# A kernel whose instruction order comes from an emission clock: SyncE's queue and each landing are put into the clock, the weight sums' rows are laid out anew and stored in two parts, and the first loads change places

## The chip, the cores and the metric

One core of one Trainium2 chip. The metric is the device time of one execution in microseconds (us), lower is better. A ratio is the mean time of one kernel's fast runs over the mean of the other's fast runs of the same rounds, so it is not quite the ratio of the medians that stand beside it. Engines in the profile: PE is TensorE's products, PEld its weight loads, DVE is VectorE, ACT is ScalarE, SP is SyncE, which issues the DMAs.

## The reference

Two layers of local attention and gated MLP over 2048 tokens, with shared weights:

```python
def reference(A_x, A_wqkv, A_wo, B_x, B_w1, B_w3, B_w2):
    # _A_ref: qkv = x @ wqkv, 32 heads of 32; each token attends to 8 tokens,
    #         2 apart, backwards; softmax; @ wo
    # _B_ref: h = silu(x @ w1) * (x @ w3); h @ w2      (1024 -> 3584 -> 1024)
    x = A_x
    x = x + _A_ref(_layernorm(x, axis=-1), A_wqkv, A_wo)
    x = x + _B_ref(_layernorm(x, axis=-1), B_w1, B_w3, B_w2)
    x = x + _A_ref(_layernorm(x, axis=-1), A_wqkv, A_wo)
    x = x + _B_ref(_layernorm(x, axis=-1), B_w1, B_w3, B_w2)
    return x
```

## The kernel before

Tokens go in four chunks of 512. Each engine executes its stream strictly in the order in which the program emits it, and that order is decided while the program is built, by a **clock of guesses**: `now` holds where TensorE, VectorE and ScalarE would stand, and VectorE's background work (norms, sums, values, scores) is emitted in front of an urgent operation only if the guess says it ends by then.

```python
    MM, TABLE, DMA = 0.216, 1.3, 2.5
    now = dict(pe=23.6, dve=15.0, act=24.5, table=None)
    x_at = [12.5, 21.5, 38.0, 44.0]          # when each chunk of x is believed there
    ...
    def background(until):
        while True:
            for queue in (norms, adds, values, scores):
                s = head(queue)
                if s is not None and max(now["dve"], s[1]) + s[0] <= until:
                    take(queue)
                    break
            else:
                return
```

A transfer is guessed by a constant: q, k and v are there 2.5 us after the later of the request and the store; a transposed tile 3.0 us after VectorE.

```python
            turned.append(max(now["dve"] + 3.0, turned[-1] + 1.5))
    ...
        qks[l, h] = qT, kT, max(now["dve"], qkv_at[l, h // R, 1]) + DMA
```

From the third unit on (a unit is one chunk of one layer), gate and up products use seven sums of weight blocks instead of eight blocks. ScalarE and VectorE make them during the first two units: a pass over the tile measures its size, a tiny product spreads the size, ScalarE writes scaled copies into a block, VectorE subtracts, and the block is stored to DRAM.

```python
        elif slot == 2:
            measure(u, g, w, junk)        # ScalarE, 3.6 us
        elif slot == 5:
            scales(u, g)                  # the "size" product on TensorE
            copies(u, g, w, 0)            # ScalarE writes block 0
    ...
    t_d = [[dram.tile([P, 2, 7 * KT // 2 * P], FP16, ...) ...]]
        nc.sync.dma_start(t_d[m][g][:, a, :], b.rearrange("p b k c -> p (b k c)"))
```

Three names recur. A *gather* is the small product with which TensorE collects the sums of scores that VectorE has made (`L` from `psm`). An *addition* is a sum of two results on VectorE for which the next `st` product, one of the gate and up products, waits (`st` from `st` and `big`). A *size product* spreads the measured size of a weight tile (`size`).

## Time and profile before

| | |
|---|---|
| median | 1632.05 us (1631.71 to 1632.39) |
| span of the profiled run | 1633.2 us |
| TensorE busy | 1586.3 us |
| VectorE busy | 1220.5 us |
| DMA share | 72% |

Three lines that the prediction does not show. The first is the page's share of the chain that ended last, by engine; the second is of ScalarE's waits (who, for what: us, times, longest); the third of the page's DMA issues (count, size of each, median us to landing).

```profile
PE 69%; DVE 18%; DMA 8%; ACT 2%; issue 1%; SPq 1%; DVEq 0%; ACTq 0%
```

```profile
ACT big L747 <- DMA t_d<-big: 21.5, 8, 7.2
```

### The profile page before, as it was taken

What the parts mean: (1) busy time and instruction counts of PE and PEld (TensorE: products, weight loads), DVE (VectorE), ACT (ScalarE), POOL (GpSimd) and SP (SyncE); (2) the same over time, 40 slices, a digit from 0 to 9 for tenths busy, and PEclk for the clock granted to TensorE, in tenths of its full rate; (3) what the DMA queues carried; (4) which work ended last, traced back from release to release, by engine and by line L of the source; (5) the groups of instructions that cost most, each with busy time, mean ns of one, the idle gap of its engine ahead of it and who ended that gap; (6) DMA issues with size and microseconds to landing.
All of it is one profiled execution on the core that took longest, in us unless ns stands there. A gap on an engine that the chain in (4) does not pass through costs nothing.

```text
span 1633.2 us, 24503 instructions
## 1 busy us (share of the span) xinstructions
PE 1586.3 (97%) x9844; PEld 1015.4 (62%) x9844; DVE 1220.5 (75%) x2180; ACT 647.9 (40%) x1002; POOL 3.4 (0%) x16
## 2 busy tenths in 40 slices
PE   9799999999899899999999999999999999999999
PEld 7566644444344477575675756757667667676866
DVE  4788887988889699898688977898389885434423
ACT  4243374546635236142452333514235223332421
POOL 0000000000000000000000000000000000000000
PEclk9999999999999999999999999999999999999999
DMA  8555758686948879577687867767878576867954
GB/s 260 158 174 133 202 179 286 187 268 192 305 136 277 268 251 286 195 260 233 217 259 238 266 222 234 241 236 250 269 216 299 193 257 219 266 232 254 318 181 143
DMA packets 298786, 377.91 MB, mean 231 GB/s; under 512 B 71472, under 2 KB 234672, under 8 KB 298544
## 3 DMA queue, kind: packets, MB, share of 16 engines
q1 hardware_dynamic: 298528, 376.22, 72.2%
q8 instruction: 77, 1.26, 0.3%
q14 instruction: 37, 0.30, 0.1%
q10 hardware_dynamic: 144, 0.13, 0.0%
HBM read 305.53 MB, written 55.05 MB: 221 GB/s over the span
## 4 chain that ended last, share of the span: by engine, by line
PE 69%; DVE 18%; DMA 8%; ACT 2%; issue 1%; SPq 1%; DVEq 0%; ACTq 0%
PE st L796 24%; PE acc L927 21%; PE ps L703 12%; PE po L651 6%; DVE tm L562 3%; DVE pr L478 3%; DMA xnT<-xn 2%; PE pg L901 2%; DVE tm L402 2%; PE pu L910 2%; DVE pr L402 2%; DMA t_d<-big 2%; DVE st L209 2%; DMA w3t<-in_B_w_dram 1%; DMA kT<-qkv_d 1%
## 5 line engine op out<-in xcount | busy, mean ns | idle before, releaser
L927 PE MATMUL acc<-w2t,hT 128*128 128x512 bf16 (+1 forms) x1804 | 391.1, 378 | 0.9 <-DMA w2t<-in_B_w_dram 0.9
L703 PE MATMUL ps<-xnT,wqkv 128*128 128x512 f16 (+1 forms) x1472 | 326.5, 383 | 0.0
L927 PEld LDWEIGHTS <-hT 128*128 128x128 bf16 x1804 | 176.2, 98 | 209.0 <-issue 1.9
L796 PEld LDWEIGHTS <-early 128*128 128x128 f16 x2688 | 263.9, 98 | 41.7 <-issue 2.0
L703 PEld LDWEIGHTS <-wqkv 128*128 128x128 bf16 x1472 | 211.1, 144 | 112.3 <-issue 7.6
L796 PEld LDWEIGHTS <-late 128*128 128x128 f16 x2016 | 197.5, 98 | 43.4 <-issue 18.9
L478 DVE TENSOR_TENSOR pr<-qT,kT 128x2048 bf16<-128x2048 bf16 x128 | 155.7, 1216 | 55.2 <-DMA kT<-qkv_d 55.2
L707 ACT CAST big<-ps 128x512 bf16<-128x512 f32 x184 | 106.2, 586 | 228.1 <-PE ps L703 222.7
L796 PE MATMUL st<-xnT,late 128*128 128x256 f16 x1344 | 175.8, 274 | 4.9 <-DVE big L844 4.6
L796 PE MATMUL st<-big,early 128*128 128x256 f16 x1344 | 173.4, 274 | 1.2 <-ACT st L822 1.2
L562 DVE TENSOR_TENSOR tm<-At,vT 128x2048 bf16<-128x2048 bf16 x128 | 155.7, 1216 | 17.2 <-ACT At L535 17.2
L796 PE MATMUL st<-xnT,early 128*128 128x256 f16 x1344 | 167.8, 274 | 0.0
L822 ACT COPY st<-st 128x512 f32<-128x512 f32 x84 | 48.2, 574 | 300.9 <-PE st L796 297.8
L937 DVE TENSOR_TENSOR x_sb<-x_sb,acc 128x512 bf16<-128x512 bf16 x129 | 87.2, 677 | 91.3 <-PE acc L927 90.6
L402 DVE TENSOR_TENSOR pr<-pr 128x1024 bf16<-128x1024 bf16 (+1 forms) x256 | 136.9, 550 | 0.4
L402 DVE TENSOR_TENSOR tm<-tm 128x1024 bf16<-128x1024 bf16 (+1 forms) x256 | 136.7, 549 | 0.3
L651 PE MATMUL po<-wo,oT 128*128 128x512 bf16 x512 | 116.9, 382 | 0.0
L910 PE MATMUL pu<-xnT,w3t 128*128 128x512 f16 x448 | 105.9, 379 | 2.5 <-DMA w3t<-in_B_w_dram 2.4
L901 PE MATMUL pg<-xnT,w1t 128*128 128x512 f16 x448 | 107.2, 382 | 0.3 <-DMA w1t<-in_B_w_dram 0.3
L834 DVE TENSOR_TENSOR st<-st,big 128x512 f32<-128x512 f32 x84 | 58.2, 693 | 63.9 <-ACT big L831 63.7
L810 DVE SCALAR_TENSOR_TENSOR hT<-st,down_scale,sg 128x512 bf16<-128x512 f32 x126 | 92.8, 744 | 12.1 <-PE st L796 12.1
L805 ACT ACTIVATE sg<-st,down_scale 128x512 bf16<-128x512 f32 x126 | 86.9, 690 | 32.5 <-PE st L796 31.8
(120 smaller groups left out, 1256.6 us busy)
## 6 DMA issues: line engine op xcount, KB each, us to landing
early<-t_d SPq DMA_DIRECT2D x84, 1024.0 KB, 7.0
late<-t_d SPq DMA_DIRECT2D x84, 768.0 KB, 6.4
w2t<-in_B_w_dram SPq DMA_DIRECT2D x48, 1024.0 KB, 7.7
wqkv<-in_A_wqkv_dram SPq DMA_DIRECT2D x28, 1024.0 KB, 7.8
t_d<-big SPq DMA_DIRECT2D x28, 896.0 KB, 5.0
qkv_d<-big SPq DMA_DIRECT2D x92, 256.0 KB, 2.5
w1t<-in_B_w_dram SPq DMA_DIRECT2D x14, 1024.0 KB, 7.6
w3t<-in_B_w_dram SPq DMA_DIRECT2D x14, 1024.0 KB, 10.1
```

What stands on the lines that cost most here:

```text
L402: nc.vector.tensor_tensor(b[:, 0:m, :], b[:, 0:m, :], b[:, m:2 * m, :], op=ALU.add)
L478: V.tensor_tensor(pr[:], qT[:], kT[:, :, k0:k0 + TCH], op=ALU.mult)
L562: V.tensor_tensor(tm[:], At[:], win, op=ALU.mult)
L651: nc.tensor.matmul(ps[:], lhsT=oT[:, t, j * P:(j + 1) * P], rhs=wo[:, t, hh * 512:(hh + 1) * 512], start=(t == 0), stop=(t == KT - 1))
L703: nc.tensor.matmul(ps[:], lhsT=ws[kk // KH][:, kk % KH, t::KT], rhs=xnT[:, kk, :], start=(kk == 0), stop=(kk == KT - 1))
L707: nc.scalar.copy(sgt[:, t - t0, :], ps[:])
L796: nc.tensor.matmul(out[:, a, :], lhsT=w[:, a, blk, k, :], rhs=rhs[:, k, :], start=start and a == 0 and k == 0, stop=k == KQ - 1, skip_grou ...
L810: nc.vector.scalar_tensor_tensor(hT[:, f:f + 2, t0:t0 + HT], src, inv, gates[g, q][:], op0=ALU.mult, op1=ALU.mult)
L901: nc.tensor.matmul(pg[:], lhsT=w1t[:, kk, fi * P:(fi + 1) * P], rhs=xnT[:, kk, :], start=(kk == 0), stop=(kk == KT - 1))
L910: nc.tensor.matmul(pu[:], lhsT=w3t[:, kk, fi * P:(fi + 1) * P], rhs=xnT[:, kk, :], start=(kk == 0), stop=(kk == KT - 1))
L927: nc.tensor.matmul(acc[:], lhsT=hT[:, f - f0, j * P:(j + 1) * P], rhs=w2ts[(f - f0) // 8][:, (f - f0) % 8, q0:q0 + step], start=(f == f0), ...
L937: nc.vector.tensor_tensor(xs, xs, acc[:], op=ALU.add)
```

## The change

The intent is that the clock know SyncE's queue and each DMA's landing, that weights, transposes, q, k and v be believed there when the queue would deliver them, that x be there early, and that the sums lie in DRAM as rows of 8 KB (early) and 6 KB (late) per partition.

```diff
-    MM, TABLE, DMA = 0.216, 1.3, 2.5
-    now = dict(pe=23.6, dve=15.0, act=24.5, table=None)
+    MM, TABLE = 0.216, 1.3
+    now = dict(pe=23.6, dve=15.0, act=24.5, table=None, sp=11.0, dma=26.0)
-    x_at = [12.5, 21.5, 38.0, 44.0]
+    x_at = [12.5, 21.5, 24.5, 27.5]
+    def dma(kb, ready=0.0, issue=0.45):
+        now["sp"] = max(now["sp"], ready, now["dma"] - 9.0) + issue
+        now["dma"] = max(now["dma"], now["sp"] + 0.2) + kb / 380
+        return now["dma"] + 1.3
 ...
-            turned.append(max(now["dve"] + 3.0, turned[-1] + 1.5))
+            turned.append(dma(420, max(now["dve"], free), 1.3))
 ...
-        load_x(1)
+        for c in range(1, NCH):
+            load_x(c)
 ...
-        qks[l, h] = qT, kT, max(now["dve"], qkv_at[l, h // R, 1]) + DMA
+        qks[l, h] = qT, kT, load_part(kT, l, 1, h * TCH, True)     # load_part returns dma(540, ...)
 ...
     def weight(kind):
+        now["pe"] = max(now["pe"], w_at[used[0]])
 ...
-        nc.sync.dma_start(t_d[m][g][:, a, :], b.rearrange("p b k c -> p (b k c)"))
+        nc.sync.dma_start(t_d[m][g][:, 4 * a:4 * (a + 1)], b[:, 0:4])
+        nc.sync.dma_start(t_d[m][g][:, 8 + 3 * a:8 + 3 * (a + 1)], b[:, 4:7])
 ...
-                then = (lambda: (load_weight(), load_weight()), lambda: load_x(2), lambda: load_x(3))
+                then = (None, lambda: (load_weight(), load_weight()))
```

Cut: `dma()` calls beside the other loads and stores, the believed time of the first q store, the loads' new views of the sums, and the bookkeeping of free transposed tiles.

More of the change, by code (lines that the diff above doesn't have):

```diff
@@ L192 @@
     down_scale = const.tile([P, 2, NG], FP32, name="down_scale")
-    t_d = [[dram.tile([P, 2, 7 * KT // 2 * P], FP16, name=f"t_d{m}_{g}") for g in range(NG)] for m in range(2)]
+    t_d = [[dram.tile([P, 14, KT // 2, P], FP16, name=f"t_d{m}_{g}") for g in range(NG)] for m in range(2)]
     qkv_d = [[dram.tile([P, KT, S], BF16, name=f"qkv_d{l}_{i}") for i in range(3)] for l in range(2)]
@@ L226, in norm_apply @@
         xnT = xnTs[key]
+        free = xnT_free.get(list(xnTs)[list(xnTs).index(key) - 2], 0.0)
         mv, sd, ready = moments[key, r]
@@ L248 @@
     turned = [0.0] * 3
+    xnT_free = {}
     moments = {}
@@ L389, in first_q @@
                     nc.sync.dma_start(q_rows[:, 4 * i:4 * i + 4, 0:CH], hT[:, 4 * i:4 * i + 4, :])
-        qkv_at[0, 0, 0] = now["act"] + DMA / 2
+        qkv_at[0, 0, 0] = 28.0
     def tree(n, mul, dst):
@@ L434, in load_part @@
             nc.sync.dma_start(tl[:], qkv_d[l][which][:, :, tok0 - (HALO if halo else 0):tok0 + TCH])
+        return dma(540, max(now["dve"] if which < 2 else 0.0, qkv_at[l, tok0 // CH, which]))
     def load_qk(l, h):
@@ L441, in load_qk @@
         load_part(qT, l, 0, h * TCH, False)
-        load_part(kT, l, 1, h * TCH, True)
-        qks[l, h] = qT, kT, max(now["dve"], qkv_at[l, h // R, 1]) + DMA
+        qks[l, h] = qT, kT, load_part(kT, l, 1, h * TCH, True)
     def load_v(l, h):
@@ L448, in load_v @@
         vT = qkvp.tile([P, KT, HALO + TCH], BF16, name="vT")
-        load_part(vT, l, 2, h * TCH, True)
-        vs[l, h] = vT, max(now["dve"], qkv_at[l, h // R, 2]) + DMA
+        vs[l, h] = vT, load_part(vT, l, 2, h * TCH, True)
     pe_queue = []
@@ L588 @@
             seq += [("qkv", which, h) for which in range(3) for h in range(2)]
-    w_tiles, due, used = [], [], [0]
+    w_tiles, w_at, due, used = [], {}, [], [0]
     def load_weight(pieces=1):
@@ L601, in load_weight @@
                                   wqkv_v[:, n * KH + k0:n * KH + k0 + step, i * D:(i + 1) * D])
+            at = dma(1024, now["pe"] if len(w_tiles) > 5 else 0.0)
         elif kind == "junk":
             w = wp.tile([P, KT, FG * P], BF16, name="junk", tag="w")
+            at = 0.0
         elif kind in ("early", "late"):
@@ L606, in load_weight @@
             w = wp.tile([P, 2, 4 if early else 3, KT // 2, P], FP16, name=kind, tag="w")
-            v = t_d[i][n][:].rearrange("p a (b k c) -> p a b k c", b=7, k=KT // 2)
-            nc.sync.dma_start(w[:], v[:, :, 0:4] if early else v[:, :, 4:7])
+            v = t_d[i][n][:, 0:8] if early else t_d[i][n][:, 8:14]
+            nc.sync.dma_start(w[:], v.rearrange("p (a b) k c -> p a b k c", a=2))
+            at = dma(1024 if early else 768, now["pe"])
         elif kind == "w2":
@@ L611, in load_weight @@
             nc.sync.dma_start(w[:, 0:n, :], w2_v[:, i:i + n, rest[0] * 512:(rest[0] + 1) * 512])
+            at = dma(128 * n, now["pe"])
         else:
@@ L615, in load_weight @@
             nc.sync.dma_start(w[:, :, 0:n * P], v[:, :, i * P:(i + n) * P])
+            at = dma(1200, now["pe"])
+        w_at[len(w_tiles)] = at
         w_tiles.append(w)
@@ L714, in q_part @@
             nc.sync.dma_start(qkv_d[l][which][:, t0:t0 + SG, c * CH:(c + 1) * CH], sgt)
+            stored = dma(256, done)
             if first and t0 == SG:
-                load_part(qT, 0, 0, 0, False)
+                first_at = load_part(qT, 0, 0, 0, False)
             between(False)
@@ L719, in q_part @@
                 then[t0 // SG]()
-        qkv_at[l, c, which] = done + DMA / 2
+        qkv_at[l, c, which] = stored
+        if which == 2:
+            xnT_free["Q", l, c] = now["pe"]
         if first:
-            qks[0, 0] = qT, kT, done + 0.1
+            qks[0, 0] = qT, kT, max(done + 0.1, first_at)
     def measure(m, g, w, junk):
@@ L758, in differences @@
         dve(1.4, r)
-        nc.sync.dma_start(t_d[m][g][:, a, :], b.rearrange("p b k c -> p (b k c)"))
+        nc.sync.dma_start(t_d[m][g][:, 4 * a:4 * (a + 1)], b[:, 0:4])
+        nc.sync.dma_start(t_d[m][g][:, 8 + 3 * a:8 + 3 * (a + 1)], b[:, 4:7])
+        dma(512, now["dve"])
+        dma(384, now["dve"])
     def prepare(u, g, slot, w1t, w3t, junk):
@@ L917, in b_stage @@
                 release(3)
+            if lastsplit:
+                xnT_free["B", l, c] = now["pe"]
             for hh in range(2):
@@ L939, in b_stage @@
                             nc.sync.dma_start(xout[:, n, o0:o0 + step], xs)
+                            dma(128, now["dve"])
                     if j == TPC - 1:
@@ L968 @@
             if c == 0 and which == 1:
-                then = (lambda: (load_weight(), load_weight()), lambda: load_x(2), lambda: load_x(3))
+                then = (None, lambda: (load_weight(), load_weight()))
             if c == 2 and which == 0:
-                then = (None, None, lambda: nc.sync.dma_start(wo[:], wo_v))
+                then = (None, None, lambda: (nc.sync.dma_start(wo[:], wo_v), dma(2048)))
             q_part(0, c, which, w_tiles[2 * which:2 * which + 2], then)
```

## The prediction

> **What bounds the kernel now.** I began with the page's busy line, then asked for the groups by shape, the waits of TensorE and VectorE, busy time in chosen windows, and the DMA issues in order of time. The page says that TensorE is the bound, and leaves 1633.2 - 1586.3 = 46.9 us of idle time on it:
>
> ```profile
> PE 1586.3 (97%) x9844; PEld 1015.4 (62%) x9844; DVE 1220.5 (75%) x2180; ACT 647.9 (40%) x1002; POOL 3.4 (0%) x16
> ```
>
> The chain that ended last gives the pace of TensorE where nothing holds it. Columns: start, length, work, instructions.
>
> ```profile
> 1411.08 27.63 PE acc L927 x128
> 1438.71 36.75 PE st L796 x336
> ```
>
> That is 0.2159 us for a 512-column product and 0.1094 us for a 256-column one. The groups by shape count, after the first query part, 1780 + 1344 + 128 + 512 + 448 + 448 + 64 + 64 = 4788 of the first kind and 4 x 1344 - 672 + 24 = 4728 of the second. **Floor**: 24.1 us until the key part starts (from the order of time), 4788 x 0.2159 = 1033.7, 4728 x 0.1094 = 517.2, about 2 for 28 tiny size products, 2.9 after the last product: 1580 us. So 53 us are to be had at most. The change removes no product.
>
> Where are the 53? Windows (columns: stretch, its length, busy us and count of PE, PEld, DVE, ACT, POOL; granted clock; DMA share; GB/s):
>
> ```profile
> 24.00:66.00 42.00, 42.00 (x200) 27.97 (x198) 21.14 (x45) 16.60 (x39) 0.00 (x0) 1.00 0.76 229
> 66.00:94.00 28.00, 19.39 (x86) 11.55 (x85) 21.79 (x41) 8.41 (x14) 0.00 (x0) 0.88 0.57 147
> 405.00:440.00 35.00, 30.62 (x136) 13.46 (x135) 29.79 (x68) 26.21 (x33) 0.00 (x0) 0.95 1.01 279
> 520.00:570.00 50.00, 45.14 (x202) 24.04 (x200) 33.44 (x62) 15.32 (x27) 0.00 (x0) 0.93 0.84 253
> 745.00:785.00 40.00, 37.54 (x170) 23.61 (x169) 27.12 (x48) 15.55 (x26) 0.00 (x0) 0.96 0.67 224
> 975.00:1015.00 40.00, 36.02 (x210) 24.07 (x209) 27.16 (x49) 14.03 (x22) 0.00 (x0) 0.91 0.74 243
> 1180.00:1220.00 40.00, 35.97 (x227) 24.80 (x226) 29.00 (x52) 14.11 (x23) 0.00 (x0) 0.91 0.73 244
> 1340.00:1600.00 260.00, 260.00 (x1938) 189.34 (x1937) 110.11 (x168) 85.89 (x139) 0.00 (x0) 1.00 0.73 248
> ```
>
> Six windows hold idle of 8.6, 4.4, 4.9, 2.5, 4.0 and 4.0 us = 28.4. Each also lost clock, width x (1 - clock): 3.4, 1.8, 3.5, 1.6, 3.6, 3.6 us, together 17.5; part of it falls inside the wait itself. The balance gives what counts: idle beyond start and end is 46.9 - 2.2 - 2.9 = 41.8, and 53 - 41.8 = about 11 us is clock. Small waits make up the other 13 us of idle. From 1340 to 1600 there is nothing to win.
>
> The causes, from the waits (who waited, for what: us, times, longest), first TensorE's, then VectorE's:
>
> ```profile
> PE st L796 <- DVE st L834: 8.9, 8, 3.1
> PE L L491 <- DVE vT L431: 8.6, 1, 8.6
> PE L L491 <- DVE psm L404: 7.3, 2, 4.9
> PE size L732 <- ACT junk L726: 5.3, 4, 3.6
> ```
>
> ```profile
> DVE pr L478 <- DMA kT<-qkv_d: 55.2, 7, 26.1
> DVE st L209 <- DMA x_sb<-in_A_x_dram: 25.9, 2, 20.4
> DVE xn L236 <- DMA xnT<-xn: 11.3, 3, 7.1
> ```
>
> TensorE waits almost never for a DMA itself. It waits for VectorE, placed by the emission clock before products that VectorE could not serve, because VectorE stood in its own in-order stream before a late transfer. At 81.2 the gather waited 8.6 us for scores that began 20 us late behind x; at 554.0 it waited 4.9 us after a transpose had sat 12.4 us in the queue; at 998 and 1200 an addition came 3 us late because VectorE had waited 10.1 and 26.1 us for k.
>
> **What the Trainium skill says.** "TensorE: Matmul & The Clock Gate", Part 1, puts a quiet TensorE at half clock after one idle window of about 3.4 us. The trace agrees in kind: the fully busy stretch has clock 1.00, the six windows 0.88 to 0.96, and even a 2.5 us wait cost clock. "DMA: Bandwidth & Descriptors", Issuing engines are not separate DMA queues, says all transfers share the same 16 engines; that agrees with four transposes queued behind four weight tiles at 531.56 taking until 548.3 (alone, at 76.6, one lands in 3.2). Its table Measured gives 6.15 us for 1 MB on another issue path; here a 1024 KB weight tile takes 5.3 us behind one small store, and early tiles have a median of 7.0, so the measured ones are used. "Perfetto Trace Analysis", Identifying the Most-Contended Engine, warns that matmul busy share is no distance from the roof; that is why I count products instead.
>
> **The change part by part.**
>
> *All x loads first.* Before, chunks 2 and 3 were issued at 41.88 and 43.17 and landed at 49.1 and 52.5. Chunk 1 landed at 20.83; a 1 MB load follows its predecessor by about 2.8 us (15.36, 18.17, 20.83), so they will land near 23.5 and 26.3, in time in which the queue idled. VectorE finishes chunk 1 at 28.7, then needs about 11 us of statistics (49.14 to 60.35 before), and reaches the scores near 40 instead of 60.35. Twenty-one us later they are done, at 61 instead of 81.2. The first wait goes: 8.6 plus about 1.5 of clock, **-10**.
>
> *v's weights behind the transposes.* This costs. Before, they were issued at 28.76 and 29.27 and landed at 34.10 and 38.05; v's products started at about 37.9, just in time. Now four transposes precede them on SyncE: the key store at 28.35, then 4 x 1.38 us (their spacing at 76.63 to 82.14) to 34.2, a store, the q load, and the weights at about 35.3 and 35.8. With 5.3 us each at least and 2.7 between them, they land at 40.5 to 42 and 43 to 45. TensorE starts v at 37.9, has only four products (0.9 us) between the two tiles, so it loses 43 to 45 minus 38.8 = 4 to 6 us, plus some 1.5 us of slow clock: **+6.5**. Nothing in the diff makes the first v part wait for a modelled arrival, so the clock does not even see this.
>
> *The modelled queue.* A k/q pair is believed there 2.5 us after its request before; the trace has 5.3 to 9.9 us to landing for k. Now score steps wait, in the emission, for modelled landings, transposes likewise; VectorE takes other work first. Idle plus clock of the stalls at 554 (4.9 + 2.3), 998 and 1200 (4.0 + 3 each) is 21 us; I expect **-17.5**. The one at 768 (2.5 + 1.6) follows a 4.5 us wait for a transposed tile: **-2.5**. The one near 429 (3.6 + 1.6) is ScalarE's chain of table loads, stores and measuring, whose release of the blocks stays unmodelled: **-1**.
>
> *Sums as 6 and 8 KB rows.* Early tiles read one run of 8 KB per partition instead of two of 4, late ones 6 instead of two of 3; stores become two of 4 and 3 KB rows instead of one of 7. The number of bytes stays. TensorE has no wait for early or late, so this is worth **0** there. It adds 28 issues of about 0.35 us on SyncE, off the path unless SyncE is already behind.
>
> *Small waits* (13 us): **-1**. *New stalls*, since every background piece moves and a schedule of 24,503 instructions is never right everywhere: **+5**.
>
> Sum: -10 + 6.5 - 17.5 - 2.5 - 1 - 1 + 5 = -20.5; 1632.05 - 20.5 = **1611 us**, 1.3% faster.
>
> **Rivals.** (1) *All stalls go and v's weights are in time*: six stalls (28.4 + 11) minus little, 1632 - 36 = 1596, over 2%. For it: each large wait traces back to a mispredicted landing. Against it: the v-weight arithmetic above, and small waits that no modelled transfer explains. (2) *The stalls move*: the new order meets other late transfers, above all around v's weights and in the two stages with DMA shares near 1.0, where a modelled wait for weights can also delay the clock too far and pack VectorE's work ahead of what TensorE needs. Then only the first 10 us and some of the rest come, and return as the v stall: about 1626. (3) *VectorE becomes the bound in the middle* (it is 85 to 95% busy there): against it, it has 1220.5 us of work in 1633, and 20 us of earlier start only helps. It would make about 1620. (4) *Transfers get faster by the longer rows*: even if they did, nothing on TensorE waits for them; no time.
>
> **Range and chances.** The hard ends are the floor of 1580 and no gain. The stall at v (2 to 9 us), the share of the modelled stalls removed (10 to 20 of 21) and new stalls (0 to 15) are independent; they put eight in ten between 1599 and 1626. Faster by over 2% needs less than about 1600, so 33 of the 53 us: 0.13. Slower by over 2% would need 33 us of new stalls: 0.01.
>
> **What would show it.** x chunks 2 and 3 land before 28 and the scores start near 40; the 8.6 us wait at the first gather is gone. A TensorE wait for v's weights of 4 to 6 us shows near 38 to 45, with clock below 1.00. VectorE's wait for k falls from 55 us to under 30, and the additions of L834 hold TensorE for under 3 us instead of 8.9. The product counts stay; early and late tiles land about as before. TensorE's idle falls from 46.9 to about 30. I am wrong if v's part starts on time (then nearer 1603), if k's waits stay on VectorE, or if a new wait over 5 us appears elsewhere.

## More of the kernel before

```profile
t_d<-big SPq DMA_DIRECT2D x28, 896.0 KB, 5.0
```

A quarter of the last chain is VectorE and DMA, although TensorE is busy 97% of the time: the chain runs through the waits. The second line is the one that the prediction passed over: ScalarE waits 21.5 us for stores of blocks that it wants to overwrite.

## The result, and the profile after

| | before | after |
|---|---|---|
| median | 1632.05 us (1631.71 to 1632.39) | 1613.4 us (1613.05 to 1613.76) |
| ratio | | 0.9886 (0.9843 to 0.9928) |
| TensorE busy in the profiled span | 1586.3 of 1633.2 | 1577.1 of 1612.0 |

In later rounds the changed kernel was measured once more: 1611.65 us, 0.9865 (0.9839 to 0.9891). The time fell by 1.1 to 1.4%. In the profile after, 71 of the 9844 product records are missing, so its busy time is a little low; in the windows below the counts of PE and PEld differ by at most three. Over the whole span the waits that the profile lists for TensorE sum to 43.7 us before and 27.9 after.

Windows of the changed kernel (stretch, length, busy us and count of PE, PEld, DVE, ACT, POOL; granted clock; DMA share; GB/s):

```profile
24.00:66.00 42.00, 35.23 (x151) 21.76 (x153) 34.34 (x70) 14.79 (x33) 0.00 (x0) 0.92 0.63 170
66.00:94.00 28.00, 28.00 (x133) 18.17 (x132) 20.22 (x35) 13.05 (x22) 0.00 (x0) 1.00 0.64 171
340.00:356.00 16.00, 13.55 (x56) 5.82 (x56) 12.57 (x26) 11.76 (x14) 0.00 (x0) 0.89 0.96 322
430.00:448.00 18.00, 13.12 (x50) 5.53 (x49) 13.19 (x28) 14.33 (x18) 0.00 (x0) 0.81 1.01 306
745.00:785.00 40.00, 40.00 (x189) 26.11 (x188) 28.57 (x48) 17.16 (x29) 0.00 (x0) 1.00 0.72 244
975.00:1015.00 40.00, 39.79 (x284) 28.74 (x287) 31.47 (x52) 17.64 (x27) 0.00 (x0) 1.00 0.78 255
```

The first two rows have changed places against before: what was full is now short by 6.8 us, what was short is full. The windows near 770 and 1000, with 2.5 and 4.0 us of idle before, are full. A new short one lies near 345. The one near 435 is not new: the wait of 3.6 us that ended at 429 before is one of 4.8 now. TensorE's waits name them, and VectorE's wait for k stands beside (who, for what: us, times, longest):

```profile
PE size L750 <- ACT junk L744: 9.4, 3, 4.8
PE ps L718 <- DMA wqkv<-in_A_wqkv_dram: 6.6, 2, 5.5
PE acc L950 <- DMA w2t<-in_B_w_dram: 2.3, 1, 2.3
PE st L817 <- DVE st L855: 1.5, 3, 0.7
```

```profile
DVE pr L486 <- DMA kT<-qkv_d: 62.4, 4, 28.3
```

The additions that let `st` products go hold TensorE for 1.5 us instead of 8.9. The first wait (6.6) is v's weights, the other is the size product behind ScalarE's measuring pass. VectorE's wait for k has not fallen: 62.4 us against 55.2.

How can the additions be in time when k is as late? Two stretches in order of time show it (start, length, instruction, in brackets the idle before and what ended it), before and after:

```profile
1188.60 1.23 DVE L478 TENSOR_TENSOR pr<-qT,kT 128x2048 bf16<-128x2048 bf16 x1 [26.08 <-DMA kT<-qkv_d]
...
1201.84 0.69 DVE L834 TENSOR_TENSOR st<-st,big 128x512 f32<-128x512 f32 x1
```

```profile
1174.16 1.23 DVE L486 TENSOR_TENSOR pr<-qT,kT 128x2048 bf16<-128x2048 bf16 x1 [28.32 <-DMA kT<-qkv_d]
...
1180.58 0.69 DVE L855 TENSOR_TENSOR st<-st,big 128x512 f32<-128x512 f32 x1
```

VectorE stands idle for k in both. Before, 13.2 us of score steps lay between k's landing and the first addition; after, 6.4 us. The clock no longer believes that score steps ran during the idle time, so it puts fewer of them ahead of the addition (the run with the old belief, below, tests this). The wait itself held up next to nothing on TensorE here.

v's weights, in the order of time of TensorE's stream:

```profile
43.41 1.93 PE L718 MATMUL ps<-xnT,wqkv 128*128 128x512 bf16 x4 [5.50 <-DMA wqkv<-in_A_wqkv_dram]
46.44 3.76 PE L718 MATMUL ps<-xnT,wqkv 128*128 128x512 bf16 x10 [1.11 <-DMA wqkv<-in_A_wqkv_dram]
```

And ScalarE's stream ahead of the longest wait of a size product, the one of 4.8 us that ended at 439.85:

```profile
430.27 1.28 ACT L220 ACT_TABLE_LOAD   x1
...
431.88 1.28 ACT L524 ACT_TABLE_LOAD   x1
...
433.82 1.28 ACT L926 ACT_TABLE_LOAD   x1
...
436.09 3.62 ACT L744 ACTIVATE junk<-w3t 128x4096 bf16<-128x4096 bf16 x1
```

Sqrt for a norm, Exp for a score and Silu for the gate each load their table, 3.8 us in sum, right in front of the measuring pass on which the size product waits.

### The profile page after: what moved, and what is told of

Same layout as the page of the kernel before. It is cut to its first block, busy times and chain, and to the rows that moved or that the text cites.

```text
span 1612.0 us, 24534 instructions
## 1 busy us (share of the span) xinstructions
PE 1577.1 (98%) x9773; PEld 1014.6 (63%) x9844; DVE 1220.5 (76%) x2180; ACT 651.0 (40%) x1002; POOL 3.4 (0%) x16
## 4 chain that ended last, share of the span: by engine, by line
PE 84%; DVE 7%; DMA 3%; ACT 3%; issue 2%; SPq 0%; ACTq 0%; DVEq 0%
PE st L817 28%; PE acc L950 24%; PE ps L718 18%; PE po L666 6%; PE pg L922 3%; PE pu L931 3%; DMA t_d<-big 1%; DVE tm L570 1%; ACT big L765 1%; DMA wqkv<-in_A_wqkv_dram 1%; DVE st L215 1%; DVE tm L411 1%; PE pq L343 1%; DVE pr L486 1%; DVE hT L831 1%
## 5 line engine op out<-in xcount | busy, mean ns | idle before, releaser
L950 PE MATMUL acc<-w2t,hT 128*128 128x512 bf16 x1764 | 390.5, 379 | 4.8 <-DMA w2t<-in_B_w_dram 2.3
L486 DVE TENSOR_TENSOR pr<-qT,kT 128x2048 bf16<-128x2048 bf16 x128 | 155.7, 1216 | 63.0 <-DMA kT<-qkv_d 62.4
L666 PE MATMUL po<-wo,oT 128*128 128x512 bf16 x486 | 113.5, 379 | 1.4
```

The source lines that it names most:

```text
L486: V.tensor_tensor(pr[:], qT[:], kT[:, :, k0:k0 + TCH], op=ALU.mult)
L666: nc.tensor.matmul(ps[:], lhsT=oT[:, t, j * P:(j + 1) * P], rhs=wo[:, t, hh * 512:(hh + 1) * 512], start=(t == 0), stop=(t == KT - 1))
L950: nc.tensor.matmul(acc[:], lhsT=hT[:, f - f0, j * P:(j + 1) * P], rhs=w2ts[(f - f0) // 8][:, (f - f0) % 8, q0:q0 + step], start=(f == f0), ...
```

## The experiments

Twelve kernels ran. Base and parts, all with medians and ratios to the kernel before of their own rounds; differences below are differences of ratios times 1634 us, or of medians within the same rounds. The runs r1 and r3 are from one chip, r2 from another, in rounds without the changed kernel itself:

| run | median us | ratio (95%) |
|---|---|---|
| r1_after: the changed kernel again | 1611.65 | 0.9865 (0.9839 to 0.9891) |
| r1_v_early | 1605.05 | 0.9824 (0.9799 to 0.9850) |
| r1_x_late | 1597.01 | 0.9779 (0.9748 to 0.9809) |
| r1_rows_old | 1623.07 | 0.9934 (0.9907 to 0.9961) |
| r2_split_store | 1611.67 | 0.9871 (0.9857 to 0.9886) |
| r2_loads_only | 1645.33 | 1.0076 (1.0060 to 1.0092) |
| r2_land_old | 1626.86 | 0.9960 (0.9942 to 0.9979) |
| r2_turn_old | 1622.31 | 0.9935 (0.9920 to 0.9951) |
| r3_two_numbers | 1630.73 | 0.9981 (0.9946 to 1.0016) |
| r3_measure_early | 1615.89 | 0.9895 (0.9866 to 0.9923) |
| r3_no_weight_wait | 1615.18 | 0.9881 (0.9849 to 0.9913) |
| r3_late_measure | 1591.69 | 0.9741 (0.9716 to 0.9766) |

The theory under test is the prediction's own, step by step; its rivals stand in what was expected of each run. First the base:

> The changed kernel unchanged, as a base for the others on this chip. Both theories: 1613 us, ratio to before 0.988, a TensorE wait of 5.5 us for v's weights at 38 and of 1.1 at 45.

It came out at 1611.65 us (1610.35 to 1613.48), with waits of 5.3 and 0.8 us for v's weights.

### What v's late weights cost

```diff
-        for c in range(1, NCH):
-            load_x(c)
+        [load_x(c) for c in range(1, NCH)]; kept = now["sp"], now["dma"]
+        load_weight(); load_weight(); now["sp"], now["dma"] = kept
...
-                then = (None, lambda: (load_weight(), load_weight()))
+                then = (None, lambda: (dma(1024), dma(1024)))      # the clock sees the same as before
```

Nothing but two DMAs on SyncE moves; the other engines' streams are identical.

> The changed kernel with v's two weight loads issued right after the x loads instead of behind the transposes; nothing else moves on any engine. Theory (the late weights cost the 6.6 us of wait and about 3 us of half clock): 1604 us, no wait at 38, clock 1.00 from 24 to 66. Rival (the transposes or the q load, now behind 2 MB of weights, make a new wait of the same size, which is why the weights were put behind): 1611 to 1615 us.

It ran in 1605.05 us (1603.91 to 1606.73), 6.6 less than the changed kernel in the same rounds, with no overlap of the single times. Its window:

```profile
24.00:66.00 42.00, 39.88 (x184) 26.17 (x186) 36.13 (x74) 17.03 (x37) 0.00 (x0) 0.99 0.73 208
```

The wait for weights is gone; a first gather now waits 2.0 us at 62, so a part of the stall's 9.5 us (6.6 idle, some 3 of clock) came back there. The time of the theory was missed by 1 us. The rival's mechanism is there but small: VectorE now waits 4.7 us for the q load behind the weights, and the gather stands behind the scores that need q; its time, 1611 us or more, fell.

### Whether x first is worth anything

```diff
-    x_at = [12.5, 21.5, 24.5, 27.5]          and dma=26.0
+    x_at = [12.5, 21.5, 49.2, 52.5]          and dma=20.6
-        for c in range(1, NCH):
-            load_x(c)
+        load_x(1)
-                then = (None, lambda: (load_weight(), load_weight()))
+                then = (lambda: (load_weight(), load_weight()), lambda: (load_x(2), dma(1024)),
+                        lambda: (load_x(3), dma(1024)))
```

> The changed kernel with the old order of loads (x chunks 2 and 3 at 42, v's weights ahead of the transposes), but its emission clock told so (arrivals 49.2 and 52.5). Theory A (x first is worth 10 us by itself, v's weights behind it cost 9.5; the gather's wait came from the wrong clock as much as from the late load): the v wait is gone and the gather does not wait 8.6 us again, 1603 to 1609 us. Theory B (late x starves VectorE by 20 us whatever the clock knows): a gather or value wait of 8 us or more comes back, 1612 to 1618 us.

1597.01 us (1596.43 to 1599.26): better than both theories, 14 us under the changed kernel. TensorE's waits, and one window:

```profile
PE size L749 <- ACT junk L743: 4.2, 4, 2.7
...
PE L L498 <- DVE vT L439: 1.2, 1, 1.2
```

```profile
240.00:580.00 340.00, 329.19 (x1543) 159.29 (x1559) 295.64 (x580) 168.41 (x227) 0.00 (x0) 1.00 0.77 245
```

With x late and the clock told of it, the first gather waits 1.2 us instead of 8.6, so early x is not needed for that. The load order therefore costs 14 us here: 6.6 are v's weights, and the rest shows as size waits (4.2 us against 9.4) and clock (1.00 in this window, 0.98 in the changed kernel of the same rounds; 0.89 and 0.81 in its two short windows near 345 and 435). This run changes load order, two arrival times and the queue's start together, so it weighs the group.

The changed kernel's order of loads, with its two arrival times, was then put alone into the kernel before:

```diff
-    x_at = [12.5, 21.5, 38.0, 44.0]
+    x_at = [12.5, 21.5, 24.5, 27.5]
-        load_x(1)
+        for c in range(1, NCH):
+            load_x(c)
-                then = (lambda: (load_weight(), load_weight()), lambda: load_x(2), lambda: load_x(3))
+                then = (None, lambda: (load_weight(), load_weight()))
```

> The kernel before with the order of loads alone changed: all x first, arrivals 24.5 and 27.5 told to its old clock, v's weights behind the transposes. Theory of the prediction (the first gather's wait, 10 us, goes; v's weights cost 9.5): 1628 to 1636 us, with waits of 5 and 1 us near 38 and 45 and the 3 us waits near 1000 and 1200 unchanged. Rival (the VectorE head start of 20 us removes later stalls too): 1615 to 1622 us.

1645.33 us, 0.76% **slower** than before, outside both expectations:

```profile
PE size L733 <- ACT junk L727: 16.4, 5, 5.6
PE st L797 <- DVE st L835: 11.9, 8, 3.4
PE ps L704 <- DMA wqkv<-in_A_wqkv_dram: 6.3, 2, 5.1
```

The first gather's wait is gone and v's weights cost what they were said to, but size products wait 16.4 us (5.3 before) and additions 11.9 (8.9 before). So this order of loads, x first and v's weights behind the transposes, costs 12 to 14 us by either clock. In the traces, each of the three size waits of the changed kernel has an Exp with its table, and the Silu table's return, just ahead of the measuring pass; with x late, the longest one (2.7 us) has Sqrt loads and no Exp. That VectorE's head start of 20 us moves Exp there is argued: the traces show Exp standing in front, and no run moved Exp alone.

Lastly the opposite half, the two arrival times alone in the kernel before:

```diff
-    x_at = [12.5, 21.5, 38.0, 44.0]
+    x_at = [12.5, 21.5, 49.2, 52.5]
```

> The kernel before with nothing but its clock's two arrival times of x chunks 2 and 3 set to what its trace shows (49.2 and 52.5 instead of 38 and 44). Theory (the first gather waited 8.6 us because the clock was wrong, not because x was late): that wait is under 2 us and the time 1621 to 1627 us. Rival (late x itself costs the time): the wait stays or moves to the next product, 1630 to 1636 us.

1630.73 us, a ratio whose interval includes 1, and inside what the rival expected. The wait fell to 5.5 us only:

```profile
PE L L491 <- DVE vT L431: 5.5, 1, 5.5
```

```profile
DVE pr L478 <- DMA qT<-qkv_d: 16.5, 1, 16.5
```

The theory fell in its number: told that x is late, the old clock puts scores first, and they then wait for q until 45.4, which that clock does not know. The run with x late has the same wait (16.9 us, until 46.2), but its clock knows the queue, and its gather waits only 1.2 us. In these runs x's times help only together with the queue's.

### What the sums' layout is worth

```diff
+    t_d[m][g] is again [P, 2, 3584]; loads take v[:, :, 0:4] or v[:, :, 4:7]
-        nc.sync.dma_start(t_d[m][g][:, 4 * a:4 * (a + 1)], b[:, 0:4])
-        nc.sync.dma_start(t_d[m][g][:, 8 + 3 * a:8 + 3 * (a + 1)], b[:, 4:7])
+        nc.sync.dma_start(t_d[m][g][:, a, :], b.rearrange("p b k c -> p (b k c)"))
```

> The changed kernel with the weight sums in DRAM in the old layout (two runs of 4 or 3 KB per partition on loading, one store of 7 KB rows instead of two). Theory (no product waits for these tiles): 1611 to 1616 us, while the early tiles' median landing goes back from 6.4 to about 7.0 us. Rival (shorter landings shorten the queue before k and the transposes): 1617 us or more.

1623.07 us, 11 us more than the changed kernel, although the order of TensorE, VectorE and ScalarE is the same. The theory fell. ScalarE's stream at the same copy, first in the run of the changed kernel beside it, then here:

```profile
336.33 2.56 ACT L765 ACTIVATE big<-w1t,up_scale 128x512 f16<-128x512 bf16 x4 [1.89 <-DMA t_d<-big]
```

```profile
341.99 2.56 ACT L765 ACTIVATE big<-w1t,up_scale 128x512 f16<-128x512 bf16 x4 [5.17 <-DMA t_d<-big]
```

The copy overwrites a block that is being stored. Which half of the change is it, the two stores or the long rows? Old rows with two stores:

```diff
+        nc.sync.dma_start(t_d[m][g][:, a, 0:2048], b[:, 0:4].rearrange("p b k c -> p (b k c)"))
+        nc.sync.dma_start(t_d[m][g][:, a, 2048:3584], b[:, 4:7].rearrange("p b k c -> p (b k c)"))
```

> The changed kernel with the old DRAM layout (loads read two runs of 4 or 3 KB per partition) but its two stores per block kept; TensorE, VectorE and ScalarE have the very same order as the changed kernel. The whole layout change undone had given 1623 against 1612. Theory S (the gain lies in the two stores: ScalarE's copies are let go when the first part has landed, and size products wait less): 1611 to 1614 us, size waits of 2.2, 2.4 and 4.9 us as in the changed kernel. Theory R (the gain lies in the longer rows of the loads, and shorter queues behind them): 1620 to 1624 us, size waits of 4 to 6 us.

1611.67 us, the time of the changed kernel. TensorE's size wait with the one store, then with two stores and old rows:

```profile
PE size L750 <- ACT junk L744: 15.2, 4, 5.7
```

```profile
PE size L750 <- ACT junk L744: 9.4, 3, 4.8
```

The rows are worth nothing in time that these runs can see: late tiles land in 6.5 us with the old rows and in 6.0 with the new (medians), but no product waits for them. What pays is that the first part of a block has landed after 3.0 us (median) and lets three of ScalarE's four copies go, where the whole took 5.0.

### Which part of the clock

q, k and v by the old constant:

```diff
-        qks[l, h] = qT, kT, load_part(kT, l, 1, h * TCH, True)
+        load_part(kT, l, 1, h * TCH, True); qks[l, h] = qT, kT, max(now["dve"], qkv_at[l, h // R, 1]) + 2.5
```

(and the same for v)

> The changed kernel, but q, k and v are believed landed 2.5 us after request again; the queue is modelled as before for all else. Theory (the additions near 985 and 1180 are again placed behind score steps that wait for k): the two waits of 3 to 4 us and their half clock come back, 14 us, 1622 to 1630 us. Rival (transposes and weights carry the gain): 1610 to 1616 us.

1626.86 us, 15.5 us more than the changed kernel in the other rounds (14.5 more than r2_split_store in the same ones, which keeps the new clock whole). The additions near 995 and 1195 hold TensorE again, as the theory says; size waits rose by 2.2 us too.

```profile
PE st L817 <- DVE big L865: 7.4, 7, 2.7
...
PE st L817 <- DVE st L855: 3.3, 4, 1.4
```

VectorE's stream at the same place as above:

```profile
1181.85 1.23 DVE L486 TENSOR_TENSOR pr<-qT,kT 128x2048 bf16<-128x2048 bf16 x1 [28.10 <-DMA kT<-qkv_d]
...
1193.94 0.70 DVE L855 TENSOR_TENSOR st<-st,big 128x512 f32<-128x512 f32 x1
```

Idle time for k is the same 28 us; but 12.1 us of score steps stand between k's landing and the addition again, as against 6.4 with the modelled landing. So it is the order behind the wait that the modelled landing changes.

Transposes by the old constant:

```diff
-            turned.append(dma(420, max(now["dve"], free), 1.3))
+            dma(420, max(now["dve"], free), 1.3); turned.append(max(now["dve"] + 3.0, turned[-1] + 1.5))
```

> The changed kernel, but the transposed tiles are believed landed by the old guess (3.0 us after VectorE, 1.5 after the one before). Theory (the gather stall of 4.9 us near 549 and that of 2.5 near 768 went because of the modelled transposes): one or both come back, 1617 to 1625 us. Rival (they went because VectorE is 20 us ahead, or because landings of q and k are known): 1610 to 1615 us.

1622.31 us, 11.4 us more (10.5 against r2_split_store). The gathers near 581 and 754 wait 3.0 and 2.7 us, as those at 549 and 768 did before:

```profile
PE L L499 <- DVE psm L413: 6.8, 3, 3.0
```

TensorE's modelled wait for weights:

```diff
-        now["pe"] = max(now["pe"], w_at[used[0]])
```

> The changed kernel whose clock lets TensorE use weights at once, as the old clock did; landings of q, k, v and of transposes stay modelled. Theory (TensorE waits under 4 us in all for weights after 50 us, so this part is worth little): 1608 to 1616 us. Rival (the clock runs ahead and places VectorE's work wrongly): 1618 us or more.

1615.18 us, ratio 0.9881 against 0.9865 in other rounds. The intervals overlap: this part is worth little, and no sign of it is settled. Its waits trade places: one size wait of 4.9 us instead of three of 9.5 in sum, and 5.7 us for w2's weights instead of 2.6.

### A better version

```diff
-        if slot == 1 and g:
-            differences(u, g - 1, 1)
-        elif slot == 2:
+        if slot == 1:
+            if g:
+                differences(u, g - 1, 1)
             measure(u, g, w, junk)
```

> The changed kernel with ScalarE's measuring pass over a weight tile placed one half step (1.7 us) earlier before the size product. Theory (size products wait because table loads for Exp and Sqrt push the measuring pass back): the three waits of 2.2, 2.4 and 4.9 us shrink by 1.7 us each, with less half clock, 1601 to 1608 us. Rival (the measuring pass is late because of the block stores, and stays so): 1610 to 1614 us.

1615.89 us, no gain: of the three size waits one fell from 2.2 to 0.7 us, one stayed at 4.2, and one grew from 2.4 to 6.1. Ahead of the longer one ScalarE's copy waited for its store:

```profile
339.69 2.56 ACT L765 ACTIVATE big<-w1t,up_scale 128x512 f16<-128x512 bf16 x4 [6.12 <-DMA t_d<-big]
```

A half step of slack does not help where ScalarE stands before a store; the theory that table loads alone cause these waits fell. The same edit on top of the old load order:

> The best so far (old order of loads with the new clock told of it, 1597 us) plus the earlier measuring pass. Theory: its size waits of 0.8, 2.7 and 0.4 us go, 1592 to 1596 us. Rival (moving the pass shifts other ScalarE work in the way): 1597 to 1601 us.

1591.69 us (1590.67 to 1592.12), 2.6% under the kernel before and the best of all. Only one size wait is left, and the earlier wait of 2.9 us for w2's weights is gone:

```profile
PE size L749 <- ACT junk L743: 2.7, 1, 2.7
```

The 1597 it is compared with are of other rounds. The largest wait it was aimed at (2.7 us) stayed; the others, 1.5 us together, went, and with the 2.9 us for w2 that makes 4.4 of the 5 us. Why w2's weights are in time now was not looked into.

## Why the prediction was right, and where it was not

The total was right (1611 against 1613.4, and 1611.65 in the later rounds); its sum was not right term by term. Errors of opposite sign cancelled, and so far the number was luck. By the runs, the load order costs some 14 us, and the clock (27) and the two stores (11) gain 38: 24 us of gain, against 19 to 22 measured. These were undone one at a time, so the sum is a rough one.

- **The bound and the floor.** Right. TensorE's products set the time: the waits that the profile lists for TensorE sum to 14.0 us in the fastest run and to 52.8 in the slowest (1645.33), the least and the most of all. The span of the best run, 1590.4, still lies some 10 us above the floor of 1580.
- **v's weights behind the transposes, +6.5.** The mechanism was right, the size low: waits of 5.5 and 1.1 us at 38 and 45 (4 to 6 were said), and clock of some 3 (1.5 was said). The loads were issued at 36.6 and 37.3, a good microsecond later than worked out, and the second landed at 46.4, where 43 to 45 was said. Moving these two loads alone regained 6.6 us, since a gather's wait of 2.0 us came back.
- **All x loads first, -10.** The mechanism was right as far as it went (the scores' first product stands at 40.8, and the gather's 8.6 us went), the value wrong. The step "20 us of earlier start only helps" failed: the load order as a whole, put at -10 + 6.5, is +12 us alone and about +14 with the new clock. Size products wait behind ScalarE in the first two units (16.4 us against 5.3, and 9.4 against 4.2); that the head start puts Exp in their way is argued, not shown. A clock that knows x to be late, and the queue, removes the gather's wait without it.
- **The modelled queue, -17.5 - 2.5.** That the modelled landings remove these stalls was right; the term was too small. Undone one at a time, known landings of q, k and v were worth 15.5 us and known transposes 11.4, 27 if they are simply added; they were never undone together. The step "VectorE takes other work first", and with it the sign "VectorE's wait for k falls from 55 us to under 30", failed: it is 62.4 us, which the prediction itself had named as a sign of being wrong. VectorE idles as before, but less is placed ahead of the addition (6.4 us of score steps instead of 13.2, and 12.1 with the old belief).
- **Sums as 6 and 8 KB rows, 0.** The term for the rows held (two stores with old rows: 1611.67). The term for the stores failed: they were counted as 28 issues off the path, and are worth 10 to 11 us. The step that failed is "nothing on TensorE waits for them". ScalarE waited 21.5 us for these stores, the size product waits for ScalarE, and the chain was not followed that far.
- **ScalarE's chain near 429, -1, and new stalls, +5.** Too small together. Size waits rose from 5.3 to 9.4 us in three places, with clocks of 0.89 and 0.81 around two of them. The rival "the stalls move" was true of these.
- **The range.** It held because of the cancellation: with the stores' 11 us and the clock's 27 known, but not the 14 of the load order, the sum would have stood near 1593, below the range.

## What to carry to other kernels

Where the order is fixed in advance, a late transfer need not cost anything (k's, 62.4 us of waiting on VectorE, cost next to nothing; v's weights, for which TensorE itself waits, did). Believing it early costs, because urgent work is placed behind work that cannot run. In this kernel modelling the landings through the queue paid, and moving the loads did not. When a load is moved, ask which engine's work moves with it. Follow a wait list through to the engine that is not the bound: a buffer that a store holds can stand two steps in front of a product, and storing it in the pieces in which it is reused releases it earlier.

## What the Trainium skill lacked or had wrong

- "DMA: Bandwidth & Descriptors", Rules for kernel authors, advises to coalesce many small transfers into a large one, with overhead prevailing under 64 KB. Here one store of 896 KB as two of 512 and 384 KB made the kernel about 10 us faster (ratios 0.9934 and 0.9871 with the same rows), since the writer that waits for the buffer is let go in parts. These parts are above that size, so this is no contradiction; the page has no word on the release of the source.
- "TensorE: Matmul & The Clock Gate", Why this matters for your kernels, asks for no idle gaps over about 3 us. A wait of 2.5 us cost clock in the kernel before (0.96 over 40 us), while waits of 2.7 and 2.9 us cost none in the run with x late (1.00 from 240 to 580, and 1.00 from 410 to 426 and from 510 to 526, around them). In r3_late_measure a wait of 2.7 us did cost clock (0.91 from 405 to 425). A wait under 3 us can do it, and of two equal ones only one did.
- "ScalarE: Activation LUTs", What ACT_TABLE_LOAD costs, gives about 2.66 us for a switch, of which 1.38 is a drain. Here a load takes 1.28 us and the next activation starts 1.3 us after the load began (430.27, then 431.57; the activation before ended at 430.25). In 56 of 62 loads of the changed kernel's trace it starts after 1.29 or 1.30 us. No drain shows.
- None of the pages used here has what an in-order stream loses when it is arranged by wrong guesses of landings: 15.5 us for q, k and v and 11.4 us for transposes in this kernel.
